# Four of twelve blocks of a gated product by Strassen's seven products on one Trainium2 core

## The chip, the core and the metric

The kernel runs on one core of a Trainium2 chip. The core has TensorE (matrix products, results in PSUM), VectorE, ScalarE and GpSimd (elementwise work), SyncE (its queue issues most DMAs), and 16 DMA engines. Each engine works through its own queue in order and waits on semaphores for the others. The metric is the device time of one execution in microseconds (us); the median of several runs counts.

## What is computed

Attention over 2 x 8 heads, then a gated feed-forward layer (this change), then a mixture of experts. The gated layer, cut from the reference:

```
rms = np.sqrt(np.mean(x * x, axis=-1, keepdims=True) + 1e-06)
xn = x / rms * rms_g                      # 1536 tokens, 512 features
g = xn @ w_gate                           # 512 x 1536
silu = g * (1.0 / (1.0 + np.exp(-g)))
val = xn @ w_val                          # 512 x 1536
return silu * val @ w_out                 # 1536 x 512
```

The weights come as 64-bit floats.

## The kernel before

**Split operands.** A float32 operand is split in two parts, hi (a rounded copy) and lo (the rest), and a product is three matmuls: hi by hi, hi by lo, lo by hi. `xh`, `xl` hold x transposed (features on partitions, four pieces k of 128) for three groups c of 512 tokens.

**The gated stage.** The 1536 gate and value features are twelve blocks i of 128. A step is a pair (i, c): `products` (L533) issues 24 matmuls of 512 columns, for z = 0 (gate) and 1 (value) twelve each (4 pieces by 3), into the PSUM tiles `ps0` and `ps1`, two buffers each. `gate1` (L556) follows one step later: VectorE multiplies `ps0` by the tokens' scale `rs` (L561), ScalarE takes SiLU (L563), VectorE multiplies by `ps1` (L565), and the result goes to `h`. So a block is 72 matmuls, and 11 blocks follow in the loop `order`.

**Unpacking.** Each weight tile of 128 x 512 comes as raw 64-bit words (`wraw`, 512 KB, `load_unit`, two buffers). `unpack` makes float32 of it in `f64t` (two buffers) and splits it: ScalarE takes the absolute value (L491); VectorE does a max (L493), an "and" with a shift (L497) and two fused operations that read the raw words and `f64t` (L499, L502); ScalarE casts to hi (L505); GpSimd subtracts for lo (L507). In a step one unit is unpacked: the gate tile of block i+1 at c = 0, the value tile at c = 1, and a tile of w_out at c = 2 (the twelve tiles of w_out, `woh` and `wol`, are done by the last block). `step1` hands the products to TensorE's queue, and then `run` interleaves the unpacking with `gate1` of the step before, one instruction group of each in turn. After it the next raw tile is loaded into the buffer just read.

**What follows.** At the last step `split_h(0)` splits 128 tokens of `h` (six casts, six subtractions). `gemm2` (L611) multiplies by w_out: per 128 tokens, twelve pieces k with three matmuls each, in order of k (L623).

**Memory.** The `big` pool holds the tiles of `woh`, `wol` (names woh0 to woh5, wol0 to wol5, two pieces each) and `h`. A later tile may take the place of an earlier one by its tag, and then waits until that one has been read.

Of the kernel before, what the change touches and what calls it, by code (L numbers as in the profile page):

```python
# [1 line left out]

# [6 lines left out]
F32 = mybir.dt.float32  # L9
# [472 lines left out]
                          s.rd[4 * k:4 * k + 4, :].rearrange("(o a) b -> o a b", o=1).to_broadcast([128, 4, 128]))  # L482


def unpack(s, raw, pool, hi, lo, eng, c=slice(0, 512)):

    nc = s.nc
    t = pool.tile([128, 512], F32, name="f64t", bufs=2)[:, c]
    raw, hi, lo = raw[:, c], hi[:, c], lo[:, c]
    b, a = raw[:, :, 0].bitcast(U32), raw[:, :, 1]  # L490
    nc.scalar.activation(t, a.bitcast(F32), AF.Abs)  # L491
    yield
    nc.vector.tensor_scalar(t, t, F64_LEAST, None, ALU.max)  # L493
# [12 lines left out]
    yield  # L506
    eng.tensor_tensor(lo, t, f(hi), ALU.subtract)  # L507


def load_unit(s, unit):  # L510

    raw = s.wpool.tile([128, 512, 2], I32, name="wraw", bufs=2)
    src = s.w_out[128 * unit[1]:128 * unit[1] + 128, :] if unit[0] == "o" else \
        s.wgv[unit[1], :, 512 * unit[2]:512 * unit[2] + 512]
    s.nc.sync.dma_start(raw.rearrange("p n t -> p (n t)"), src.bitcast(I32))
    s.wraw[unit] = raw


def split_unit(s, unit, eng, c=slice(0, 512)):
    raw = s.wraw[unit]  # L520
    if unit[0] == "o":
        hi, lo = s.woh[unit[1]], s.wol[unit[1]]
    else:
        _, i, z = unit
# [5 lines left out]
    return unpack(s, raw, s.wpool, hi, lo, eng, c)  # L530


def products(s, i, c, a, b):  # L533

    nc = s.nc
    ps = s.gp.setdefault((i, c, a, b), [])
    for z in range(2):
        if z == len(ps):
            ps.append(s.ps_g.tile([128, b - a], F32, name=f"ps{z}", bufs=2))
        p = ps[z]  # L540
        wh, wl = s.w[i, z]
# [503 lines left out]
def attn_moe_kernel(ctx, tc, qx, kx, vx, rel, ints, wgv, w_out, rms_g, w9, w9t, w1, w2, out):  # L1045
# [20 lines left out]
    s.gpool = pool(phase2, "g")  # L1066
    early = pool(phase2, "early")
    s.apool = pool(actx, "attn")
    s.xh, s.xl, s.wraw, s.w, s.rs, s.h, s.gp = {}, {}, {}, {}, {}, {}, {}

    def htiles(pool, c, qs):
        for q in qs:
# [96 lines left out]
    places = [(i, 2, 0, 512) for i in range(1, 11)] + [(11, 0, 0, 512), (11, 1, 0, 512)]  # L1169
    for n, x in enumerate(places):  # L1170
        todo.setdefault(x, []).append(("o", n))
    ahead = iter([unit for x in order for unit in todo.get(x, ())])

    mean(s, ss, 6, 12)
    some(s.first, 24)
# [11 lines left out]
        load_unit(s, next(ahead))  # L1187
    some(second, 18)
    run(products(s, 0, 2, 0, 512))
    for x in ((0, 0, 512), (1, 0, 256), (1, 256, 512)):  # L1190
        run(gate1(s, 0, *x))
    behind = [(0, 2, 0, 512)]
    rctx.close()
    actx.close()
    big = pool(phase2, "big")
    s.woh, s.wol = [], []
    for part, tiles in (("h", s.woh), ("l", s.wol)):
        for i in range(6):
            w = big.tile([128, 2, 512], F32R, name=f"wo{part}{i}", bufs=1)
            tiles += [w[:, 0, :], w[:, 1, :]]  # L1200
    htiles(big, 0, range(1, 6))
    htiles(big, 1, range(1, 6))
    htiles(big, 2, range(6))
    def step1(x, *parts):

        run(products(s, *x))
        run(*parts, *[gate1(s, *behind.pop()) for _ in behind[:1]])
        behind.append(x)

    for x in order:  # L1210
        if x == order[1]:
            octx.close()
# [12 lines left out]
    run(gate1(s, *behind.pop()))  # L1225
    phase1.close()


# [358 lines left out]
```

## Time and profile before

| | us |
|---|---|
| median of three runs | 524.77 (523.03 to 525.8) |
| the profiled execution | 523.36 |
| its span, first to last instruction | 521.4 |
| eleven blocks of the gated stage in it | 179.5 |
| granted TensorE clock, mean | 0.995 |

The span is one execution; the 2.0 us around it are not in the trace. Times in the rows below count from the span's start. A row of a timeline is start, duration, engine, line, operation, output and inputs; the bracket is how long the engine sat idle before it, and what ended that.

### The profile page before, as it was taken

What the parts mean: (1) busy time and instruction counts of PE and PEld (TensorE: products, weight loads), DVE (VectorE), ACT (ScalarE), POOL (GpSimd) and SP (SyncE); (2) the same over time, 40 slices, a digit from 0 to 9 for tenths busy, and PEclk for the clock granted to TensorE, in tenths of its full rate; (3) what the DMA queues carried; (4) which work ended last, traced back from release to release, by engine and by line L of the source; (5) the groups of instructions that cost most, each with busy time, mean ns of one, the idle gap of its engine ahead of it and who ended that gap; (6) DMA issues with size and microseconds to landing.
All of it is one profiled execution on the core that took longest, in us unless ns stands there. A gap on an engine that the chain in (4) does not pass through costs nothing.

```text
span 521.4 us, 9740 instructions
## 1 busy us (share of the span) xinstructions
PE 506.5 (97%) x3389; PEld 414.3 (79%) x3389; DVE 396.1 (76%) x989; ACT 264.9 (51%) x620; POOL 147.1 (28%) x201
## 2 busy tenths in 40 slices
PE   8999999999999999999999999999999999999993
PEld 6776878888888888888888877877898788887772
DVE  5899895688887877777764567767746899999961
ACT  3899992433333232332332525425523599888850
POOL 2577680122222122121221000000010713666001
PEclk9999999999999999999999999999999999999998
DMA  7997611323323233232227213313784699999300
GB/s 252 391 364 269 253 43 43 143 81 121 122 80 122 81 100 103 82 116 87 93 70 255 89 41 121 122 40 123 234 298 161 208 403 397 399 402 380 134 16 17
DMA packets 32417, 89.34 MB, mean 171 GB/s; under 512 B 3876, under 2 KB 4272, under 8 KB 32361
## 3 DMA queue, kind: packets, MB, share of 16 engines
q1 hardware_dynamic: 27592, 76.36, 41.1%
q0 software_dynamic: 2896, 9.14, 4.9%
q10 hardware_dynamic: 1872, 3.15, 1.7%
q8 instruction: 29, 0.48, 0.4%
q14 instruction: 28, 0.22, 0.1%
HBM read 80.93 MB, written 8.53 MB: 172 GB/s over the span
## 4 chain that ended last, share of the span: by engine, by line
PE 77%; DVE 2%; issue 1%; ACT 1%; DMA 0%; another core or an unknown queue 0%; POOLq 0%; POOL 0%; ACTq 0%
PE ps L545 34%; PE px L623 17%; PE eph L920 8%; PE epy L953 8%; PE eht L940 1%; PE lg L598 1%; PE half L545 1%; PE po L545 1%; DVE w9b L606 1%; PE pxt L589 1%; DVE hl L577 1%; PE x L1352 1%; PE eph L991 1%; PE jy L991 1%; PE ext L906 1%
## 5 line engine op out<-in xcount | busy, mean ns | idle before, releaser
L545 PE MATMUL ps<-xh,wh 128*128 128x512 f32 x272 | 106.2, 390 | 0.0
L545 PE MATMUL ps<-xl,wh 128*128 128x512 f32 x272 | 106.1, 390 | 0.0
L545 PE MATMUL ps<-xh,wl 128*128 128x512 f32 x272 | 106.0, 390 | 0.0
L880 DVE TENSOR_TENSOR ewl<-eraw,ewh 128x1024 fp32r<-128x1024 f32 x72 | 83.7, 1221 | 9.1 <-ACT ewh L871 8.9
L871 ACT CAST ewh<-eraw 128x1024 fp32r<-128x1024 f32 x72 | 71.3, 1057 | 5.1 <-DVE ewl L880 4.9
L623 PE MATMUL px<-woh,hh 128*128 128x512 f32 (+1 forms) x156 | 61.3, 393 | 0.0
L545 PEld LDWEIGHTS ps<-xh,wl 128*128 128x128 f32 x272 | 51.1, 188 | 10.5
L545 PEld LDWEIGHTS ps<-xl,wh 128*128 128x128 f32 x272 | 51.1, 188 | 10.4
L545 PEld LDWEIGHTS ps<-xh,wh 128*128 128x128 f32 x272 | 51.1, 188 | 10.3
L623 PE MATMUL px<-woh,hl 128*128 128x512 f32 (+1 forms) x156 | 58.5, 375 | 0.0
L623 PE MATMUL px<-wol,hh 128*128 128x512 f32 (+1 forms) x156 | 58.3, 373 | 0.0
L505 ACT CAST wh<-f64t 128x512 fp32r<-128x512 f32 (+1 forms) x25 | 15.1, 604 | 84.1 <-DVE f64t L502 84.1
L507 POOL TENSOR_TENSOR wl<-f64t,wh 128x512 fp32r<-128x512 f32 (+1 forms) x24 | 29.9, 1248 | 98.0 <-ACT wh L505 61.9
L493 DVE TENSOR_SCALAR f64t<-f64t 128x512 f32<-128x512 f32 (+1 forms) x37 | 36.9, 997 | 16.8 <-ACT f64t L491 16.8
L268 ACT ACTIVATE es<-es,m 128x192 f32<-128x192 f32 (+1 forms) x96 | 41.2, 434 | 4.5 <-DVE m L257 4.3
L285 POOL TENSOR_SCALAR es<-es,z 128x192 f32<-128x192 f32 (+1 forms) x94 | 36.9, 411 | 22.6 <-DVE z L277 9.4
L577 DVE TENSOR_TENSOR hl<-h,hh 128x256 fp32r<-128x256 f32 x72 | 25.4, 423 | 17.8 <-ACT hh L576 17.8
L565 DVE TENSOR_TENSOR h<-sg,ps 128x512 f32<-128x512 f32 x34 | 23.3, 684 | 19.2 <-PE ps L545 17.2
L623 PEld LDWEIGHTS px<-woh,hl 128*128 128x128 f32 x156 | 29.3, 188 | 5.6
L623 PEld LDWEIGHTS px<-woh,hh 128*128 128x128 f32 x156 | 29.4, 188 | 5.5 <-issue 0.8
L623 PEld LDWEIGHTS px<-wol,hh 128*128 128x128 f32 x156 | 29.4, 189 | 4.2
L1365 POOL DMA_INDIRECT early<-xm,si_f x1 | 1.3, 1297 | 106.8 <-DMA eraw<-in_w_dram 106.8
(234 smaller groups left out, 1004.4 us busy)
## 6 DMA issues: line engine op xcount, KB each, us to landing
eraw<-in_w_dram SPq DMA_DIRECT2D x62, 512.0 KB, 8.9
wraw<-in_wgv_dram SPq DMA_DIRECT2D x24, 512.0 KB, 3.6
vp<-in_vx_dram SPq DMA_DIRECT2D x16, 512.0 KB, 6.0
wraw<-in_w_out_dram SPq DMA_DIRECT2D x12, 512.0 KB, 3.4
eraw<-in_w_dram POOLq DMA_DIRECT2D x10, 512.0 KB, 7.0
kd<-in_kx_dram SPq DMA_DIRECT2D x7, 464.0 KB, 10.1
vp<-in_vx_dram SPq DMA_DIRECT2D x8, 384.0 KB, 4.7
xm<-x SPq DMA_DIRECT2D x12, 256.0 KB, 2.6
```

The lines of the kernel that those rows point to most:

```text
L268: nc.scalar.activation(e[:, r, e0:e0 + n], e[:, r, e0:e0 + n], AF.Exp, bias=m[:, j:j + 1], scale=-1.0, accum_out=z[:, j:j + 1])
L285: eng.tensor_scalar(e[:, r, e0:e0 + n], e[:, r, e0:e0 + n], z[:, j:j + 1], one[0], ALU.mult, *one[1:])
L493: nc.vector.tensor_scalar(t, t, F64_LEAST, None, ALU.max)
L507: eng.tensor_tensor(lo, t, f(hi), ALU.subtract)
L545: nc.tensor.matmul(p, lhsT=w[:, k, :], rhs=x[c][:, k, a:b], start=n == 0, stop=n == 11)
L565: nc.vector.tensor_tensor(u, sg, ps[1], ALU.mult)
L577: nc.vector.tensor_tensor(hl[:, i, :], src, f(hh[:, i, :]), ALU.subtract)
L623: nc.tensor.matmul(p, lhsT=h[:, k, :], rhs=w[k][:, c:c + N], start=n == 0, stop=n == 35)
L871: eng.copy(wh, raw)
L880: eng.tensor_tensor(wl, raw, f(wh), ALU.subtract)
L920: nc.tensor.matmul(self.p[half], lhsT=x[:, k, :], rhs=w[:, 512 * half:512 * half + 512], start=k == n == 0, stop=k == 3 and n == 2)
L953: nc.tensor.matmul(self.y, lhsT=h[:, k, :], rhs=w[:, c], start=n == 0, stop=n == 23)
```

## The change

In blocks 4 to 7 the groups c = 0 and c = 1 are computed together as a 2 x 2 by 2 x 2 product of blocks (gate and value by two halves of the features; two halves of the features by two token groups), in Winograd's form of Strassen's method: seven products of six matmuls instead of eight. Group c = 2 stays as it was, its 24 matmuls set between the seven.

- `Seven.blocks` builds the four sums of x's pieces, restored as hi + lo: 24 VectorE additions of 128 x 512 and 8 ScalarE casts, in 18 portions set among blocks 0 to 3.
- `Seven.sums` builds four sums of a block's weights from its two `f64t` tiles: four VectorE operations of 256 columns, a ScalarE cast and a VectorE subtraction of 1024, in the step before.
- `Seven.quad` is the block. ScalarE copies three partial sums from PSUM to PSUM (`b<-a`, `c<-a`, `d<-a`) and one to `e`, and TensorE goes on adding to the copies.
- w_out is no longer unpacked in blocks 1 to 7: two tiles in each of blocks 8, 9 and 10 and six in block 11. Its raw tiles take other tiles' places: o0 to o3 those of h05 and h15, o4, o6, o8 that of woh5, o5, o7, o9 that of wol5, o10 and o11 the ordinary buffers. A tile that takes a place in use is loaded once its forerunner has been unpacked.

The core of the diff:

```diff
-def unpack(s, raw, pool, hi, lo, eng, c=slice(0, 512)):
+def unpack(s, unit, raw, pool, hi, lo, eng, c=slice(0, 512)):
 
     nc = s.nc
-    t = pool.tile([128, 512], F32, name="f64t", bufs=2)[:, c]
+    s.full[unit] = pool.tile([128, 512], F32, name="f64t", bufs=2)
+    t = s.full[unit][:, c]
     raw, hi, lo = raw[:, c], hi[:, c], lo[:, c]
...
+SEVEN = range(4, 8)
+class Seven:
+    def __init__(self, s, big):
+        self.s, self.big, self.s7 = s, big, {}
+        self.th = [self.tile(f"th{j}", f"woh{j + 1}", F32R) for j in range(4)]
+        self.tl = [self.tile(f"tl{j}", f"wol{j + 1}", F32R) for j in range(4)]
+        self.eg = self.tile("eg", "wol5", F32)
...
+    def blocks(self):
+        s, V = self.s, self.s.nc.vector
+        m = [self.tile(f"tm{j}", tag, F32) for j, tag in enumerate(("h05", "h15", "h25", "woh5"))]
+        where = ((1, 0), (0, 0), (1, 2), (0, 2))
+        def full(j, k):
+            c, k0 = where[j]
+            V.tensor_tensor(m[j][:, k, :], f(s.xh[c][:, k0 + k, :]), f(s.xl[c][:, k0 + k, :]), ALU.add)
+        def sub(out, a, b, k):
+            V.tensor_tensor(m[out][:, k, :], m[a][:, k, :], m[b][:, k, :], ALU.subtract)
+        def high(j, out, k):
+            s.nc.scalar.copy(self.th[j][:, k, :], m[out][:, k, :])
+        def low(j, out, k):
+            V.tensor_tensor(self.tl[j][:, k, :], m[out][:, k, :], f(self.th[j][:, k, :]), ALU.subtract)
+        for j in range(4):
+            full(j, 0)
+            yield
+        for k in range(2):
+            for j in range(4 * k):
+                full(j, 1)
+                if j % 2:
+                    yield
+            sub(1, 0, 1, k)
+            yield
+            sub(0, 0, 2, k)
+            high(0, 1, k)
+            yield
+            sub(2, 2, 1, k)
+            high(2, 0, k)
+            low(0, 1, k)
+            yield
+            sub(3, 3, 2, k)
+            high(1, 2, k)
+            low(2, 0, k)
+            yield
+            high(3, 3, k)
+            low(1, 2, k)
+            yield
+            low(3, 3, k)
+            yield
+    def sums(self, i):
+        s, V = self.s, self.s.nc.vector
+        t0, t1 = (s.full["w", i, z] for z in range(2))
+        a = self.tile("s7", "woh0", F32).rearrange("p a b -> p (a b)")
+        a11, a12, a21, a22 = t0[:, 0:256], t0[:, 256:512], t1[:, 0:256], t1[:, 256:512]
+        S = [a[:, 256 * j:256 * j + 256] for j in range(4)]
+        V.tensor_tensor(S[0], a21, a22, ALU.add)
+        V.tensor_tensor(S[1], S[0], a11, ALU.subtract)
+        yield
+        V.tensor_tensor(S[2], a21, a11, ALU.subtract)
+        V.tensor_tensor(S[3], a12, S[1], ALU.subtract)
+        yield
+        tags = (("h05", "h15"), ("h25", "woh5"))[i % 2]
+        hi, lo = (self.tile(f"s7{x}", tag, F32R).rearrange("p a b -> p (a b)") for x, tag in zip("hl", tags))
+        s.nc.scalar.copy(hi, a)
+        yield
+        V.tensor_tensor(lo, a, f(hi), ALU.subtract)
+        self.s7[i] = [x.rearrange("p (j k m) -> p j k m", j=4, k=2) for x in (hi, lo)]
+        yield
+    def group(self, out, w, x, start=False):
+        n = 0
+        for k in range(2):
+            for a, b in ((w[0], x[0]), (w[0], x[1]), (w[1], x[0])):
+                self.s.nc.tensor.matmul(out, lhsT=a[:, k, :], rhs=b[:, k, :], start=start and n == 0,
+                                        stop=n == 5, skip_group_check=not start)
+                n += 1
+    def quad(self, i):
+        s, nc, V = self.s, self.s.nc, self.s.nc.vector
+        A = [[w[:, k:k + 2, :] for w in s.w[i, z]] for z in range(2) for k in (0, 2)]
+        both = self.s7.pop(i)
+        S = [[w[:, j] for w in both] for j in range(4)]
+        T = [[self.th[j], self.tl[j]] for j in range(4)]
+        X = {(c, k): [x[c][:, k:k + 2, :] for x in (s.xh, s.xl)] for c in range(2) for k in (0, 2)}
+        ua, ub = (s.h[c, i // 2][:, i % 2, :] for c in range(2))
+        e, sgb = self.eg[:, 0, :], self.eg[:, 1, :]
+        third = products(s, i, 2, 0, 512)
+        b, c, d = self.seeded
+        a = s.ps_m.tile([128, 512], F32, name="qa", tag="misc", bufs=1)
+        q = s.ps_g.tile([128, 512], F32, name="qe", tag="ps1", bufs=2)
+        self.group(a, A[0], X[0, 0], True)
+        self.group(q, S[0], T[0], True)
+        yield 0
+        nc.scalar.copy(b, a)
+        yield 1
+        nc.scalar.copy(e, q)
+        some(third, 8)
+        self.group(a, S[1], T[1])
+        yield 2
+        nc.scalar.copy(c, a)
+        self.group(b, A[1], X[0, 2])
+        yield 3
+        V.tensor_tensor(ua, b, s.rs[0], ALU.mult)
+        yield 4
+        sga = s.gpool.tile([128, 512], F32, name="sg", bufs=2)
+        nc.scalar.activation(sga, ua, AF.Silu)
+        some(third, 8)
+        self.group(a, S[2], T[2])
+        yield 5
+        nc.scalar.copy(d, a)
+        self.group(c, S[3], X[1, 2])
+        yield 6
+        V.tensor_tensor(ub, c, e, ALU.add)
+        V.tensor_tensor(e, a, e, ALU.add)
+        V.tensor_tensor(ub, ub, s.rs[1], ALU.mult)
+        yield 7
+        nc.scalar.activation(sgb, ub, AF.Silu)
+        some(third, 8)
+        self.group(d, A[3], T[3])
+        nc.gpsimd.tensor_tensor(ub, sgb, e, ALU.mult)
+        yield 8
+        V.tensor_tensor(ua, sga, d, ALU.mult)
...
+    places = [*((i, c) for i in range(8, 11) for c in (1, 2)), *((11, n // 2) for n in range(6))]
+    for n, p in enumerate(places):
+        todo.setdefault((*p, 0, 512), []).append(("o", n))
...
+    seven = Seven(s, big)
+    blocks = seven.blocks()
+    seven.seeded = [*(s.ps_n.tile([128, 512], F32, name="qb", tag="rb", bufs=2) for _ in range(2)),
+                    ps_o.tile([128, 512], F32, name="qd", tag="po", bufs=1)]
+    for x, n in (((0, 0, 512), 2), ((1, 0, 256), 1), ((1, 256, 512), 1)):
+        parts = gate1(s, 0, *x)
+        next(parts)
+        some(blocks, n)
+        next(parts, None)
+    behind = [(0, 2, 0, 512)]
+    s.gp[2, 0, 0, 512] = seven.seeded[0:2]
+    s.gp[2, 1, 0, 512] = [seven.seeded[2], s.ps_m.tile([128, 512], F32, name="qa", tag="misc", bufs=1)]
...
+    def load_o(*ns):
+        for n in ns:
+            tag = ("h05", "h15", "h05", "h15", "woh5", "wol5", "woh5", "wol5", "woh5", "wol5", None, None)[n]
+            load_unit(s, ("o", n), big if tag else None, tag)
+    after_o = {n: n + 2 for n in (0, 1, 4, 5, 6, 7)}
...
+    def step7(i):
+        q, (u0, u1) = seven.quad(i), (split(("w", i + 1, z)) for z in range(2))
+        next(q)
+        run(*[gate1(s, *behind.pop()) for _ in behind[:1]])
+        some(u0, 1)
+        some(u1, 1)
+        sums = seven.sums(i + 1) if i + 1 in SEVEN else iter(())
+        next(q)
+        some(u0, 4)
+        load_ahead()
+        next(q)
+        some(u0, 2)
+        some(u1, 4)
+        next(q)
+        load_ahead()
+        some(u1, 2)
+        some(sums, 2)
+        next(q)
+        some(sums, 1)
+        next(q)
+        third = gate1(s, i, 2, 0, 512)
+        next(third)
+        some(sums, 1)
+        next(q)
+        next(q)
+        next(q)
+        next(third, None)
+        next(q, None)
+    steps = dict(zip([(1, 0), (1, 1), (1, 2), (2, 0), (2, 1), (2, 2), (3, 0), (3, 1), (3, 2)], (1, 1, 3, 1, 1, 3, 1, 1, 9)))
...
+        i, c = x[:2]
+        if i in SEVEN:
+            if c == 0:
+                step7(i)
+                if i == 6:
+                    load_o(0, 1)
+            continue
...
-        step1(x, *[split_unit(s, unit, nc.gpsimd) for unit in todo.get(x, ())])
+        parts = [split(unit) for unit in todo.get(x, ())]
+        if (i, c) in steps:
+            parts.append(islice(blocks, steps[i, c]))
+        if (i, c) == (SEVEN[0] - 1, 2):
+            parts.append(seven.sums(SEVEN[0]))
+        step1(x, *parts)
         for unit in todo.get(x, ()):
-            unit = next(ahead, None)
-            if unit:
-                load_unit(s, unit)
+            if unit[0] == "w":
+                load_ahead()
+            elif unit[1] in after_o:
+                load_o(after_o[unit[1]])
+        if (i, c) in ((8, 2), (10, 2)):
+            load_o(*((4, 5) if i == 8 else (10, 11)))
```

## Rows read from the trace of the kernel before

**Rows 1.** The page: busy time of each engine, share of the span, instructions.
```profile
PE 506.5 (97%) x3389; PEld 414.3 (79%) x3389; DVE 396.1 (76%) x989; ACT 264.9 (51%) x620; POOL 147.1 (28%) x201
```

**Rows 2.** The chain that ended last, in order of time: start, us, what.
```profile
98.57 179.52 PE ps L545 x792
278.09 9.54 PE px L623 x42
```

**Rows 3.** Windows: us; busy (instructions) of PE, PEld, DVE, ACT, POOL; PEclk, DMA, GB/s.
```profile
163.90:180.20 16.30, 16.30 (x73) 13.51 (x72) 12.59 (x18) 5.13 (x9) 3.90 (x3) 1.00 0.30 95
261.80:278.10 16.30, 16.30 (x73) 13.50 (x72) 10.60 (x19) 6.82 (x17) 2.61 (x2) 1.00 0.22 61
```

**Rows 4.** Timeline of VectorE, one step of the stage.
```profile
174.84 0.69 DVE L565 TENSOR_TENSOR h<-sg,ps 128x512 f32<-128x512 f32 x1 [0.54 <-PE ps L545]
175.44 0.42 DVE L497 TENSOR_SCALAR f64t<-f64t 128x512 uint32<-128x512 uint32 x1
175.89 0.69 DVE L499 SCALAR_TENSOR_TENSOR f64t<-wraw,f64t 128x512 uint32<-128x512 uint32 x1
176.62 0.69 DVE L502 SCALAR_TENSOR_TENSOR f64t<-wraw,f64t 128x512 uint32<-128x512 uint32 x1
177.49 0.69 DVE L561 TENSOR_TENSOR h<-ps,rs 128x512 f32<-128x512 f32 x1 [0.17 <-PE ps L545]
178.58 1.05 DVE L493 TENSOR_SCALAR f64t<-f64t 128x512 f32<-128x512 f32 x1 [0.40 <-ACT f64t L491]
```

**Rows 5.** Timeline of ScalarE, the same step and the end of the stage.
```profile
177.34 0.62 ACT L505 CAST woh<-f64t 128x512 fp32r<-128x512 f32 x1 [3.68 <-DVE f64t L502]
177.87 0.67 ACT L491 ACTIVATE f64t<-wraw 128x512 f32<-128x512 f32 x1
178.43 0.64 ACT L563 ACTIVATE sg<-h 128x512 f32<-128x512 f32 x1
...
272.69 1.94 ACT L576 CAST hh<-h 128x256 fp32r<-128x256 f32 x6 [1.30 <-PE ps L545]
```

**Rows 6.** Timeline of GpSimd, the same step and one earlier.
```profile
178.04 1.30 POOL L507 TENSOR_TENSOR wol<-f64t,woh 128x512 fp32r<-128x512 f32 x1 [4.03 <-ACT woh L505]
...
77.68 1.01 POOL L415 TENSOR_TENSOR sq<-sq 128x256 f32<-128x256 f32 x1 [0.37 <-ACT sq L424]
```

**Rows 7.** Timeline of VectorE, earlier.
```profile
78.13 1.10 DVE L499 SCALAR_TENSOR_TENSOR f64t<-wraw,f64t 128x512 uint32<-128x512 uint32 x1
...
106.88 0.68 DVE L561 TENSOR_TENSOR h<-ps,rs 128x512 f32<-128x512 f32 x1
...
111.64 0.68 DVE L561 TENSOR_TENSOR h<-ps,rs 128x512 f32<-128x512 f32 x1
```

**Rows 8.** The tile wraw: time from DMA issue to landing.
```profile
DMA to landing us min/median/max: 3.2/3.5/3.8
```

**Rows 9.** Waits of the DMA queue of SyncE: total us, times, longest.
```profile
SPq L515 <- DVE f64t L502: 149.9, 30, 9.3
```

**Rows 10.** Timeline of VectorE, end of the stage.
```profile
273.36 2.10 DVE L577 TENSOR_TENSOR hl<-h,hh 128x256 fp32r<-128x256 f32 x6
...
278.19 0.69 DVE L565 TENSOR_TENSOR h<-sg,ps 128x512 f32<-128x512 f32 x1 [2.10 <-PE ps L545]
```

**Rows 11.** Groups by line, engine and shape: count, busy us, mean ns, idle before.
```profile
L880 DVE TENSOR_TENSOR ewl<-eraw,ewh 128x1024 fp32r<-128x1024 f32 x72 | 83.7, 1221 | 9.1 <-ACT ewh L871 8.9
L871 ACT CAST ewh<-eraw 128x1024 fp32r<-128x1024 f32 x72 | 71.3, 1057 | 5.1 <-DVE ewl L880 4.9
...
L930 ACT ACTIVATE eh<-eph 128x512 f32<-128x512 f32 x16 | 8.7, 605 | 5.5 <-issue 5.5
```

**Rows 12.** Semaphore instructions of line 565 on VectorE: ns min/median/max.
```profile
L565 DVEq EVENT_SEMAPHORE  x34: 21/21/21, 103.3 to 278.1; - x34
```

**Rows 13.** Timeline of TensorE, last product of the stage.
```profile
277.70 0.39 PE L545 MATMUL ps<-xh,wl 128*128 128x512 f32 x1
```

More of the change, by code (lines that the diff above doesn't have):

```diff
@@ L1 @@
 from contextlib import ExitStack
+from itertools import islice
 import concourse.bass as bass
@@ L507, in unpack, with load_unit @@
     eng.tensor_tensor(lo, t, f(hi), ALU.subtract)
-def load_unit(s, unit):
-    raw = s.wpool.tile([128, 512, 2], I32, name="wraw", bufs=2)
+def load_unit(s, unit, pool=None, tag=None):
+    raw = (pool or s.wpool).tile([128, 512, 2], I32, name="wraw", tag=tag or "wraw", bufs=1 if tag else 2)
     src = s.w_out[128 * unit[1]:128 * unit[1] + 128, :] if unit[0] == "o" else \
@@ L529, in split_unit @@
             s.w[i, z] = [x.rearrange("p (k m) -> p k m", k=4) for x in (hi, lo)]
-    return unpack(s, raw, s.wpool, hi, lo, eng, c)
+    return unpack(s, unit, raw, s.wpool, hi, lo, eng, c)
 def products(s, i, c, a, b):
@@ L547, in products, with tile @@
                 yield
+SEVEN = range(4, 8)
[5 more added lines that the diff above has]
+        self.eg = self.tile("eg", "wol5", F32)
+    def tile(self, name, tag, dtype):
+        return self.big.tile([128, 2, 512], dtype, name=name, tag=tag, bufs=1)
+    def blocks(self):
[108 more added lines that the diff above has]
+        V.tensor_tensor(ua, sga, d, ALU.mult)
@@ L1068, in attn_moe_kernel @@
     s.apool = pool(actx, "attn")
-    s.xh, s.xl, s.wraw, s.w, s.rs, s.h, s.gp = {}, {}, {}, {}, {}, {}, {}
+    s.xh, s.xl, s.wraw, s.full, s.w, s.rs, s.h, s.gp = {}, {}, {}, {}, {}, {}, {}, {}
     def htiles(pool, c, qs):
@@ L1168, in attn_moe_kernel @@
     todo = {(i, c, 0, 512): [("w", i + 1, c)] for i in range(1, 11) for c in range(2)}
-    places = [(i, 2, 0, 512) for i in range(1, 11)] + [(11, 0, 0, 512), (11, 1, 0, 512)]
-    for n, x in enumerate(places):
-        todo.setdefault(x, []).append(("o", n))
     ahead = iter([unit for x in order for unit in todo.get(x, ())])
+    places = [*((i, c) for i in range(8, 11) for c in (1, 2)), *((11, n // 2) for n in range(6))]
+    for n, p in enumerate(places):
+        todo.setdefault((*p, 0, 512), []).append(("o", n))
     mean(s, ss, 6, 12)
@@ L1189, in attn_moe_kernel @@
     run(products(s, 0, 2, 0, 512))
-    for x in ((0, 0, 512), (1, 0, 256), (1, 256, 512)):
-        run(gate1(s, 0, *x))
-    behind = [(0, 2, 0, 512)]
     rctx.close()
@@ L1195, in attn_moe_kernel, with split, load_ahead @@
     big = pool(phase2, "big")
[L1196 to L1203, printed above, removed]
+    s.woh, s.wol = {}, {}
+    for c in range(3):
+        htiles(big, c, range(c < 2, 5))
+    seven = Seven(s, big)
[10 more added lines that the diff above has]
+    s.gp[2, 1, 0, 512] = [seven.seeded[2], s.ps_m.tile([128, 512], F32, name="qa", tag="misc", bufs=1)]
+    def split(unit):
+        if unit[0] == "o" and unit[1] % 2 == 0:
+            for part, tiles in (("h", s.woh), ("l", s.wol)):
+                w = big.tile([128, 2, 512], F32R, name=f"wo{part}{unit[1] // 2}", bufs=1)
+                tiles[unit[1]], tiles[unit[1] + 1] = w[:, 0, :], w[:, 1, :]
+        return split_unit(s, unit, nc.gpsimd)
+    def load_ahead():
+        unit = next(ahead, None)
+        if unit:
+            load_unit(s, unit)
+    def load_o(*ns):
[3 more added lines that the diff above has]
+    after_o = {n: n + 2 for n in (0, 1, 4, 5, 6, 7)}
     def step1(x, *parts):
@@ L1208, in step1 @@
         behind.append(x)
-    for x in order:
-        if x == order[1]:
-            octx.close()
+    def step7(i):
[27 more added lines that the diff above has]
+    steps = dict(zip([(1, 0), (1, 1), (1, 2), (2, 0), (2, 1), (2, 2), (3, 0), (3, 1), (3, 2)], (1, 1, 3, 1, 1, 3, 1, 1, 9)))
+    for x in order:
+        i, c = x[:2]
[5 more added lines that the diff above has]
+            continue
+        if x == (10, 0, 0, 512):
+            for z in range(3):
+                htiles(big, z, (5,))
         if x == order[-1]:
@@ L1219, in attn_moe_kernel @@
             split_h(s, 0)
[L1220 to L1224 removed]
+        parts = [split(unit) for unit in todo.get(x, ())]
[4 more added lines that the diff above has]
+        step1(x, *parts)
+        for unit in todo.get(x, ()):
+            if unit[0] == "w":
[4 more added lines that the diff above has]
+            load_o(*((4, 5) if i == 8 else (10, 11)))
     run(gate1(s, *behind.pop()))
+    octx.close()
     phase1.close()
```

## The prediction

> **What bounds the kernel now.** I read the page first: TensorE is busy 97% of the span, every other engine well below [rows 1]. Then the chain that ended last: from 98.57 us the 792 matmuls of blocks 1 to 11 stand in it as one piece of 179.52 us, 226.7 ns each, and the w_out products follow at once, 42 in 9.54 us [rows 2]. The windows by block say the same: TensorE is full in each 16.3 us, at a granted clock of 1.00, which is the 2.4 GHz level [rows 3]. So a matmul less is worth 226.7 ns as long as nobody makes TensorE wait, and the question is who could. VectorE is next with 12.59 of 16.3 us in an ordinary block, and 10.60 in the last [rows 3].
>
> The timelines show how one step runs. VectorE does L565, L497, L499, L502, then waits 0.17 us for TensorE, does L561 and L493, and waits again [rows 4]: it keeps pace with TensorE and has about 1.2 us to spare in a step of 24 x 0.2267 = 5.44 us. Operations of 512 columns take 0.69 us and 0.42 (L497), and one may begin 0.60 us after an independent one [rows 4]. ScalarE does cast, absolute value and SiLU of 0.62 to 0.67 us, starting 0.53 to 0.56 apart [rows 5]. GpSimd's lo takes 1.30 [rows 6].
>
> Two more things are to be seen. L493 is of L497's kind and size, but took 1.05 us: it began at 178.58 while GpSimd worked from 178.04 to 179.34, and ended 0.29 after it [rows 4, 6]. L499, with two inputs in SBUF, normally 0.69, took 1.10 where GpSimd was at work until 78.69 [rows 6, 7]. So both kinds stand still until GpSimd's operation is over. Second, a raw tile lands 3.2 to 3.8 us after its issue [rows 8], and its issue waits for L502, the last reader of the buffer [rows 9]; with one unit a step and two buffers, 10.9 us apart, this is hidden before.
>
> **The change, part by part.**
>
> *Matmuls.* Seven groups of six instead of eight, in four blocks: 4 x 6 = 24 fewer, 24 x 0.2267 = -5.44 us. Operands and shapes are as before, so I keep the price.
>
> *Inside a block of seven* I lay the queues out in the order of the code, each instruction starting when its engine is free and its inputs are there (the walk). TensorE needs 66 x 0.2267 = 14.96 us. VectorE: two unpackings 2 x (0.42 + 0.42 + 0.69 + 0.69) = 4.44, seven operations of 512 columns 4.83, four of 256 at 0.42 (six, overlapping, take 2.10 [rows 10]) 1.68, one of 1024 at 1.22 [rows 11]: 12.2, and about 0.65 standing behind GpSimd: 12.9, so 2.1 us spare. ScalarE: two absolute values, two casts, three SiLUs, four copies near 0.605 and a cast of 1.06 [rows 5, 11]: 7.9 us. Each of the three copies from PSUM to PSUM ends 2.2 to 2.3 us before TensorE writes its source or adds to its copy, because eight matmuls of the third group stand between. No row has a copy that writes PSUM. The nearest are 0.605 for one reading it and, far off, 1.06 for twice the size [rows 11]; at either it is in time, so I take 0. If the cover went, TensorE would wait what the copy is late.
>
> *Preparation.* 24 additions of 0.69 (16.6 us) and 8 casts go into blocks 0 to 3; the first four fill VectorE's waits for SiLU in block 0, the rest stand where w_out's unpacking was (2.85 us a block as the rows have it [rows 4]). VectorE starts behind: its L561 at 106.88 has its twelve matmuls since 98.57 + 12 x 0.2267 = 101.3, so it is 5.6 us late, and it catches up 0.7 a step (4.76 us from L561 to L561, of 5.44) [rows 7]. With the additions it is 6.7 us behind in block 1 and 1.3 by the end of block 3. TensorE waits only when a PSUM tile of two steps ago is unread, at about 7.4 us behind: cost 0, with 0.7 to spare. The sums for block 4 are ready about 2 us before the second group of seven wants them. The loads of o0 and o1 stand in SyncE's queue until block 6 has read its sums; behind them wait only raw tiles of block 9, wanted a block later. PSUM: the banks used for the copies stood empty here.
>
> *w_out's tiles, moved.* This is where I expect the saving to go. Blocks 1 to 7 lose a unit each; blocks 8, 9, 10 have four units instead of three, and block 11 six instead of two. VectorE's work in blocks 8 to 10 is 4 x 2.22 + 6 x 0.69 = 13.0, some 1.5 standing behind GpSimd, and waits for `f64t`, which with two buffers frees only when GpSimd has made lo: about 17.1 us a block against 16.32, so it falls back 0.8 us a block. That alone is hidden.
>
> Block 11 is not. Call 0 the time at which its first matmul starts; without waits the w_out products would start at 16.32. The raw tiles of o6 to o9 pass through two places in turn. VectorE has read o5 at 0.8. Only then o7 is loaded and lands at 4.35 (3.45 after the issue). Its absolute value stands ahead of SiLU in ScalarE's queue, and SiLU ahead of L565 on VectorE: L565 of step (10, 2) ends at 6.3. Two "ands" and four fused operations follow, o7 is read at 9.35, and o9 lands at 12.9. The same again: L565 of (11, 0) ends at 14.8, o9 is read at 17.9, L561, SiLU and L565 of (11, 1) end at 19.9, while TensorE could have finished the block at 16.32. TensorE waits 1.25 us in step (11, 2), for `ps1` unread since (11, 0). The first piece of `split_h(0)`, cast at 19.45, holds the w_out products back by 1.93 more; its subtraction, behind GpSimd's lo of o9, by 0.96. The remaining pieces start 0.31 to 0.35 us apart (six in 1.94 and 2.10 [rows 5, 10]), faster than TensorE takes them. Then o10 and o11: their lo come at 27.7 and 29.0, a little after pieces 10 and 11 want them: 0.31 and 0.58. Sum 1.25 + 1.93 + 0.96 + 0.31 + 0.58 = +5.03 us. The second w_out product then finds its operands, and what is loaded after the stage waits for nothing that TensorE needs soon.
>
> What this hangs on: at a landing of 3.2 instead of 3.45 us in each turn the loss is 0.5 smaller. With GpSimd blocking nobody, 2.3 smaller. With one semaphore instruction of 21 ns [rows 12] more on each VectorE operation, 1.5 larger. L561's wait of 0.17 us after TensorE's end [rows 4], and 0.10 at the last L565 (matmul 277.70 + 0.39, start 278.19 [rows 10, 13]), are my price for a hand-over; twelve of them in the four blocks, unhidden, would be 12 x 0.17 = 2.0, and hidden 0, which I take.
>
> On the standing still, the rows give a sum of 5.03, and without it 2.7. The Trainium skill, "SBUF — State Buffer", section "Who interferes with whom", says that a VectorE operation in a two-port mode, or with two SBUF inputs against a GpSimd operation that reads SBUF, and GpSimd hold a port pair exclusively, and the second fully blocks. By that rule 5.03 holds; the rows of L493 and L499 agree with it (1.05 and 1.10 us instead of 0.42 and 0.69).
>
> **Sum.** 523.36 - 5.44 + 5.03 = 522.95 against the profiled execution. That execution lies 1.4 us under the median of the three runs, so for a median I lean a little upward: 523.5.
>
> **The rivals.**
>
> *Forecast: the saving is paid back in block 11.* 523.5, with 521 to 526 from the bounds above. For it: two places for six raw tiles, each turn some 8.5 us (from 0.8 to 9.35 to 17.9) where a step is 5.44. Against it: the chain has some 25 links, and 0.1 us on each would be 2.5 us.
>
> *VectorE keeps up, and most of the saving stays.* If the tiles of o6 to o9 were turned over a little faster and the subtractions fell between VectorE's operations, TensorE would wait 2.7 us or less; with no wait at all 523.36 - 5.44 = 517.9. So 518 to 520.7. For it: VectorE's own work in block 11 due before the w_out products is 4 x 2.22 and three `gate1` of 1.38, 13.0 us of 16.32, so the loss is order and not work. Against: the rows of L493 and L499.
>
> *VectorE becomes the bound in the four blocks of seven: slower.* Its place is the end of each block: five operations on the last groups come after the sixth group, and the next block's unpacking and sums stand behind them. It has 2.1 us to spare; from there every further microsecond costs TensorE one per block. At 3.1 (each of its 20 operations 0.155 us longer, or five more GpSimd blocks of 0.65) it costs 4 x 1.0: 527. For it: three GpSimd operations per block, one of them new, and most of VectorE's operations have two inputs in SBUF, the kind that stands still. Against: the walk shows only 0.65 of blocking.
>
> *Block 11 is worse than walked.* With the 21 ns, the 2.0 of hand-overs and the 3.8 us landing (+0.7): 522.95 + 4.2 = 527.
>
> A time outside: the removal of the 24 matmuls is a count, so 517.9 is a floor for the profile.
>
> **How the numbers follow.** I take 0.5% (2.6 us) as what a measurement of this kernel can tell from no change. Forecast 0.48, all within 0.5%. VectorE keeps up 0.27: faster. VectorE bounds the four blocks 0.13, block 11 worse than walked 0.12: slower together 0.25. Range: from 519.3, leaving out the lower half of the second case, to 527.8, a little past the 527 of the two slower ones; forecast's own 521 to 526.
>
> **What the profile after would show.** Blocks 4 to 7 of 14.96 us each, with no idle TensorE: then the first step and the hidden copies are right; longer blocks with waits on ScalarE or VectorE mean the third case. TensorE idle about 5 us in all between the last c = 2 product and the end of the first w_out product, its releasers L565, L576, L577 and L507: the forecast. VectorE's waits in block 11 should be on ScalarE's L491 and that on a DMA. Less than 3 us there would make me wrong downward, more than 8 upward. L499 and L502 with a mean above 0.69 show the blocking; if they stay at 0.69 beside GpSimd's lo, that part is wrong.

## The result, and the profile after

The changed kernel takes 526.16 us, the median of 15 runs (525.3 to 527.08), beside 523.12 for the kernel before in the same comparison (15 runs, 522.93 to 525.8). The ratio is 1.0053, 95% interval 1.0043 to 1.0063: slower by 0.5%, 3.0 us. The profiled execution has a span of 524.6 us [before 521.4] and took 526.1 us. The forecast was 523.5, no change that can be measured, and what came is a change clear of the noise. The time lies in the whole range, but just above the forecast's own 521 to 526.

The page's line of engines answers to [rows 1]:

```profile
PE 503.5 (96%) x3365; PEld 408.8 (78%) x3365; DVE 418.2 (80%) x1037; ACT 283.8 (54%) x648; POOL 153.6 (29%) x205
```

There are the 24 matmuls less, and VectorE has 22 us more to do. Where the time went is seen in the windows, one for each block, from its first matmul to the next block's first (columns as in [rows 3]). Shown are blocks 3, 5, 10 and 11:

```profile
130.81:147.13 16.32, 16.32 (x74) 13.51 (x72) 15.21 (x25) 6.30 (x10) 2.82 (x2) 1.00 0.20 64
162.31:177.51 15.20, 15.20 (x68) 12.39 (x66) 14.65 (x21) 7.74 (x14) 3.88 (x3) 1.00 0.23 71
...
240.57:256.89 16.32, 16.32 (x74) 13.51 (x72) 12.68 (x21) 6.46 (x11) 5.14 (x4) 1.00 0.10 34
256.89:278.65 21.76, 17.09 (x73) 13.17 (x71) 13.57 (x25) 7.61 (x14) 5.34 (x5) 1.00 0.35 122
```

Three things are to be seen. Blocks 1 to 3 cost what they cost before, so the preparation is hidden. The blocks of seven take 15.20 us (the first 15.18) and not 14.96, with no idle TensorE and the granted clock at 1.00: 60.78 us for the four instead of 65.28, a gain of 4.50 and not 5.44. And block 11 takes 21.76 us. TensorE's timeline shows where it stands still; the figure in brackets is its idle time (the third is that of the first matmul with w_out, the fourth that of the first one that takes `hl`):

```profile
267.54 0.39 PE L547 MATMUL ps<-xh,wl 128*128 128x512 f32 x1
268.12 0.50 PE L547 MATMUL ps<-xh,wh 128*128 128x512 f32 x1 [0.19 <-DVE h L702]
...
270.76 0.39 PE L547 MATMUL ps<-xh,wl 128*128 128x512 f32 x1
274.01 0.50 PE L547 MATMUL ps<-xh,wh 128*128 128x512 f32 x1 [2.87 <-DVE h L706]
274.35 0.39 PE L547 MATMUL ps<-xl,wh 128*128 128x512 f32 x1
...
278.65 0.50 PE L764 MATMUL px<-woh,hh 128*128 128x512 f32 x1 [1.62 <-ACT hh L717]
278.99 0.39 PE L764 MATMUL px<-wol,hh 128*128 128x512 f32 x1
280.04 0.50 PE L764 MATMUL px<-woh,hl 128*128 128x512 f32 x1 [0.66 <-DVE hl L718]
```

A wait costs a little more than its bracket, because the matmul behind it also starts late (274.01 to 274.35 instead of 0.227 later). Counted from start to start, less the 0.227 of a matmul, the places cost 0.46, 3.14, 1.90 and 0.94 us, and two more in the first w_out product (`wol` of o10 and o11) 0.25 and 0.57: 7.26 us in all. The brackets alone, with 0.29 for the last of the six, add up to 5.63.

The account, from the starts of matmuls: block 1 begins at 98.17 instead of 98.41 (-0.24), the blocks of seven -4.50, block 8 +0.02, the standing still +7.26, of which the kernel before has nothing. Sum +2.54; at the end of the w_out products the kernel is 2.64 us behind, and at the last matmul of the program 2.58. What lies behind that last matmul, 0.1 to 0.6 us, I did not follow.

The chain that ended last, in order of time, runs through block 11 like this (start, us, what):

```profile
257.84 0.70 DVE f64t L504
258.57 0.03 issue
258.60 3.80 DMA wraw<-in_w_out_dram
262.44 0.04 issue
262.48 0.66 ACT f64t L493
263.14 0.53 ACT sg L704
263.70 0.04 DVE h L706
263.74 0.56 issue
264.30 0.49 DVE f64t L499 x2
264.79 0.18 issue
264.97 1.29 DVE f64t L501 x2
266.26 0.61 DVE f64t L504
266.89 0.63 ACT woh L507
267.53 4.46 DMA wraw<-in_w_out_dram
272.02 0.04 issue
272.06 0.66 ACT f64t L493
272.72 0.53 ACT sg L704
```

That is the ring of two places as the prediction walked it: o5 read (L504), o7 landing, its absolute value (L493) ahead of SiLU (L704) and of the gate's product (L706), o7 read, o9 landing. The matmul that waited 2.87 us waits for the next L706, at 273.27. The tile `wraw` in this stretch has landings of

```profile
DMA to landing us min/median/max: 3.5/4.1/5.7
```

where [rows 8] had 3.2/3.5/3.8.

### The profile page after: what moved, and what is told of

Read it like the earlier page. It is cut to its first block, busy times and chain, and to the rows that moved or that the text cites. A ratio compares the mean times of both kernels' runs of the same rounds, so it can differ in the third digit from the quotient of the medians.

```text
span 524.6 us, 9769 instructions
## 1 busy us (share of the span) xinstructions
PE 503.5 (96%) x3365; PEld 408.8 (78%) x3365; DVE 418.2 (80%) x1037; ACT 283.8 (54%) x648; POOL 153.6 (29%) x205
## 4 chain that ended last, share of the span: by engine, by line
PE 39%; DVE 5%; issue 2%; DMA 2%; ACT 2%; POOL 1%; another core or an unknown queue 0%; POOLq 0%; ACTq 0%; SPq 0%
PE px L764 16%; PE eph L1061 9%; PE epy L1094 8%; DMA wraw<-in_w_out_dram 2%; DVE hl L718 1%; PE lg L739 1%; PE eht L1081 1%; DVE w9b L747 1%; DVE f64t L501 1%; PE pxt L730 1%; PE x L1565 1%; PE eph L1132 1%; PE jy L1132 1%; PE ext L1047 0%; POOL wol L509 0%
## 5 line engine op out<-in xcount | busy, mean ns | idle before, releaser
L547 PE MATMUL ps<-xh,wh 128*128 128x512 f32 x192 | 75.4, 393 | 3.1 <-DVE h L706 2.9
L547 PE MATMUL ps<-xh,wl 128*128 128x512 f32 x192 | 75.0, 391 | 0.0
L547 PE MATMUL ps<-xl,wh 128*128 128x512 f32 x192 | 75.0, 391 | 0.0
L509 POOL TENSOR_TENSOR wl<-f64t,wh 128x512 fp32r<-128x512 f32 (+1 forms) x24 | 31.7, 1319 | 100.6 <-ACT wh L507 70.2
L547 PEld LDWEIGHTS ps<-xh,wh 128*128 128x128 f32 x192 | 36.0, 188 | 11.1 <-DVE h L706 3.3
L547 PEld LDWEIGHTS ps<-xh,wl 128*128 128x128 f32 x192 | 36.1, 188 | 7.5
L547 PEld LDWEIGHTS ps<-xl,wh 128*128 128x128 f32 x192 | 36.1, 188 | 7.3
L495 DVE TENSOR_SCALAR f64t<-f64t 128x512 f32<-128x512 f32 (+1 forms) x37 | 24.4, 662 | 18.4 <-ACT f64t L493 18.2
L718 DVE TENSOR_TENSOR hl<-h,hh 128x256 fp32r<-128x256 f32 x72 | 26.7, 440 | 11.3 <-ACT hh L717 11.3
L493 ACT ACTIVATE f64t<-wraw 128x512 f32<-128x512 f32 (+1 forms) x37 | 23.6, 651 | 11.4 <-DMA wraw<-in_w_out_dram 6.0
```

What stands on the lines that cost most here:

```text
L718: nc.vector.tensor_tensor(hl[:, i, :], src, f(hh[:, i, :]), ALU.subtract)
```

## Experiments

**e1: half of w_out.** The second half of w_out's tiles isn't loaded or taken apart, and pieces 6 to 11 of the w_out products use the tiles of 0 to 5; everything else is the changed kernel. The values after the stage, and with them the routing, are others, so only the stage is read.

```
-    for n, p in enumerate(places):
+    for n, p in enumerate(places[:6]):
...
+            for n in range(6):
+                s.woh[n + 6], s.wol[n + 6] = s.woh[n], s.wol[n]
```

> The six units of w_out in block 11 are left out: pieces 6 to 11 of the w_out products read the tiles of pieces 0 to 5, so the values behind the stage differ, the routing sees other data, and only the gated stage and the first w_out product are to be read. Theory A (the loss is the late unpacking in block 11): TensorE has no gap over 0.3 us from the first product of block 1 to the end of the first w_out product; the stage and that product together take 4.5 us less than before, instead of 2.8 us more. Theory B (the loss is made before block 11, in the blocks of seven or by VectorE's lag): gaps of 3 us or more stay.

Its block 11, 256.95 to 273.27, takes 16.32 us with TensorE busy throughout, and no matmul of the stage or of the w_out products waits. The last of the w_out products starts at 390.99 us instead of 398.32: 7.3 us earlier than in the changed kernel. So what the change loses there comes with the six units of w_out in block 11, all of it. The six units in blocks 8 to 10 are still taken apart here, and by themselves they cost nothing.

**e2: without the copies in PSUM.** The three copies b, c, d are left out and each group starts its PSUM tile afresh, so the sums are not handed over and the values are others; only the blocks of seven are read.

```
-        nc.scalar.copy(b, a)
...
-        self.group(b, A[1], X[0, 2])
+        self.group(b, A[1], X[0, 2], True)
...
```

> In the blocks of seven the three copies from PSUM to PSUM are left out, and the groups that would add to a copy start afresh, so the values are others and only blocks 4 to 7 are read. They took 15.2 us each after the change, 14.96 at 226.7 ns a matmul. Theory C (the hand-overs from ScalarE cost this, with every wait met in time): they fall to 14.96 to 15.0. Theory D (it comes from something else, such as the other operands or the change of group): they stay at 15.2, to 0.05.

The blocks take 15.20 us as with the copies, and each matmul has the same distance to the next as in the changed kernel, to 2 ns. So the 0.24 us a block is no hand-over of the copies and no wait for ScalarE's copies. (This run's block 1 begins 2.7 us late, before anything that the edit touches; its 528.58 us says nothing of the copies.) The copies themselves take 0.57 to 0.58 us, just under the nearer of my two bounds, and are hidden.

**e3: the move alone.** Blocks 4 to 7 with eight products as before, but w_out's tiles late and in two places, as in the changed kernel; the preparation runs and is not used.

```
-        if i in SEVEN:
-            if c == 0:
-                step7(i)
...
-            continue
...
```

> Blocks 4 to 7 are ordinary again (72 matmuls, no sums of weights); x's four sums are still built and w_out is unpacked as late as in the change. Theory A: the move alone costs its 7.2 us: 523.1 + 7 = 530, 528 to 531, with TensorE idle about 7 us in block 11 and the first w_out product. Theory B: within 1.5 us of before, 523 to 524.5.

529.91 us (529.14 to 530.56), ratio 1.0124 (1.0105 to 1.0143), before 523.06: the move costs 6.9 us by itself. It has TensorE's clock to show as well. Windows from block 11's start to the end of its long wait, and from there to the first w_out product:

```profile
261.54:277.89 16.35, 13.76 (x62) 11.07 (x60) 9.09 (x17) 5.44 (x9) 3.89 (x3) 1.00 0.47 161
277.89:282.53 4.64, 4.61 (x13) 3.32 (x13) 3.94 (x8) 2.19 (x5) 1.49 (x2) 0.63 0.00 2
```

After a wait of 2.59 us the granted clock is 0.63, so the 1.2 GHz level in part of the stretch, and seven matmuls in a row come 0.43 us apart. In the changed kernel's profile it stayed at 1.00 after 2.87 us. It did not make the first w_out product late: that took 20.99 us from block 11's start here and 21.76 there, and here too TensorE waited for the first cast piece of `h` (idle for 0.04 us in front of it). That this is one kernel's single profile against another's leaves open what decides the clock.

**e4: four places.** o6 and o7 get places of their own and are loaded in block 8, so only o8 and o9 wait for a place.

```
-            tag = (... "woh5", "wol5", "woh5", "wol5", "woh5", "wol5", None, None)[n]
+            tag = (... "woh5", "wol5", "woh4", "wol4", "woh5", "wol5", None, None)[n]
...
-    after_o = {n: n + 2 for n in (0, 1, 4, 5, 6, 7)}
+    after_o = {0: 2, 1: 3, 4: 8, 5: 9}
...
-            load_o(*((4, 5) if i == 8 else (10, 11)))
+            load_o(*((4, 5, 6, 7) if i == 8 else (10, 11)))
```

> o6 and o7 get places of their own (those of woh4 and wol4, free after block 7), so that o6 to o9 are loaded a block or a step earlier; order and work of all engines stay. Theory A, ring part (most of the loss is the wait for o7 and o9 to land): gaps in block 11 and the first w_out product fall from 7.25 to about 3.5 us, 526.2 - 3.7 = 522.5, 521.5 to 523.5. If the loss is VectorE's work in block 11 and not the landing: within 1 us of 526.2.

522.77 us (522.26 to 523.32), ratio 0.9991 (0.9981 to 1.0001): 3.4 us under the changed kernel's 526.16, which is what the ring of two places was worth. Both waits for PSUM tiles are gone. What is left, TensorE's groups by line from 256 to 300 us (busy, mean ns | idle before, releaser):

```profile
L764 PE MATMUL px<-woh,hh 128*128 128x512 f32 x32 | 12.9, 403 | 1.5 <-ACT hh L717 1.5
L764 PE MATMUL px<-wol,hh 128*128 128x512 f32 x32 | 12.7, 397 | 0.3 <-POOL wol L509 0.3
L764 PE MATMUL px<-woh,hl 128*128 128x512 f32 x31 | 12.2, 394 | 0.7 <-DVE hl L718 0.7
```

are the waits for the first pieces of h.

**e5: the gate first.** Two places as in the change, but in blocks 8 to 11 the queues get the gate operations ahead of the unit of w_out.

```
-        run(*parts, *[gate1(s, *behind.pop()) for _ in behind[:1]])
+        gate = [gate1(s, *behind.pop()) for _ in behind[:1]]
+        run(*(gate + list(parts) if x[0] >= 8 else list(parts) + gate))
```

> The changed kernel with one order turned round: in blocks 8 to 11 VectorE and ScalarE get the gate operations of the step before first and the unit of w_out behind them. The two places of o4 to o9 stay. Theory A (in block 11 the loss is order: SiLU and the product with it stand behind an absolute value that waits for a late raw tile, so a late load also holds TensorE's PSUM tiles): TensorE no longer waits in block 11, about 3.7 us of the 7.25 go, 526.2 - 3.7 = 522.5, range 521.5 to 523.5. Rival B (the ring itself is the limit, whoever stands first: a raw tile is then read later, o7 and o9 land later, and what block 11 gains the first w_out products lose): 525 to 527, with the waits moved from ps1 to the pieces of w_out.

521.26 us (521.11 to 522.39), ratio 0.9962 (0.9949 to 0.9975), a little below the range expected. The tiles are late as before, but nothing that TensorE needs stands behind them: the waits for `ps1` are gone, and 3.1 us are left in front of the pieces of h and of `wol`.

**e6: both.**

> Both at once: four places for o4 to o9 and the gate ahead of the unit in blocks 8 to 11. Theory A (the two causes are the whole of the loss in block 11): with four places alone 3.5 us of TensorE's gaps are left between the last product and the first w_out products, of which the walk leaves 0 to 0.5 with both; 522.8 - 3.0 to 3.5 = 519.3 to 519.8, range 518.8 to 520.5, faster than the kernel before by about 3.5 us. It doesn't reach 518.0, because the blocks of seven stay at 15.2 us. Rival B (VectorE's work in block 11 is the limit, and order only moves the wait): 522 to 523, with the same 3.5 us of gaps, now in front of the pieces of w_out's last tiles.

519.0 us (518.58 to 519.87), ratio 0.9924 (0.9911 to 0.9938). Block 11 is full again:

```profile
256.97:273.29 16.32, 16.32 (x73) 13.52 (x72) 13.72 (x27) 9.29 (x19) 5.99 (x5) 1.00 0.28 96
```

VectorE has 13.72 us of work there, as much as with the waits (13.57): it was never too much work. The order and the places were the whole of the 7.26 us.

**e7 to e10: what makes the blocks of seven 15.20.** e7 gives every group of six the first group's operands; e8 is the kernel before with the two PSUM tiles of a product taking turns every 6 matmuls. In e7, e9 and e10 the values of these blocks are others, so only the length of the blocks is read and not the time.

```
+        A = [[w[:, 0:2, :] for w in s.w[i, 0]] for _ in range(4)]
+        S = A
+        T = [[x[0][:, 0:2, :] for x in (s.xh, s.xl)] for _ in range(4)]
+        X = {(c, k): T[0] for c in range(2) for k in (0, 2)}
...
```

> Only the stage of blocks 4 to 7 is to be read: every group of six there takes the same weights and the same piece of x (those of the first group), so the sums and x's restored pieces are made and not used and the values of these blocks are others. Order, PSUM tiles, copies and waits of the groups stay. Theory A (the 0.24 us that each block of seven takes beyond 66 x 226.7 ns comes from its operands, where they lie in SBUF): the blocks fall to 14.96. Rival B (it comes from how short the runs of matmuls into one PSUM tile are, six and eight instead of twelve): they stay at 15.20.

```
+    runs = (range(2), range(2, 4)) if i else (range(4),)
+    order = [(z, k) for ks in runs for z in range(2) for k in ks]
+    for z, k in order:
...
```

> The kernel before with one edit, which leaves the result as it is: in blocks 1 to 11 the two PSUM tiles of a product take turns every 6 matmuls instead of every 12. Theory B (short runs into one PSUM tile cost TensorE time): a block takes more than 16.32 us, at the cadence of the blocks of seven 72 x 230.3 ns = 16.58, so 11 x 0.26 = +2.9 us, 526 (525 to 527). Rival A (the operands, not the runs): 16.32 us a block and 523.1 (522.5 to 523.8).

e7's blocks of seven take 14.96 us:

```profile
192.20:207.16 14.96, 14.96 (x67) 12.39 (x66) 10.82 (x16) 6.89 (x13) 3.90 (x4) 1.00 0.21 71
```

In e8 blocks 2 to 11 stay at 16.32. Its time, 524.13 us (524.02 to 527.39), is 0.9 above the kernel before, not the expected 2.9: block 1 alone takes 17.33, with a wait of 0.7 for a PSUM tile that is now wanted six matmuls earlier. Short runs cost nothing; the operands do. Which of them, with e6 as the base:

```
-        T = [[self.th[j], self.tl[j]] for j in range(4)]
+        T = [[x[c][:, k:k + 2, :] for x in (s.xh, s.xl)] for c in range(2) for k in (0, 2)]
```

> Only the stage of blocks 4 to 7 is to be read (the values there are others). The kernel with four places and the gate first; its groups take pieces of x itself where they took x's restored pieces, and keep the weights' sums. Theory A1 (the restored pieces as moving operand cost the 0.24 us a block): 14.96 to 15.0 us a block. Rival A2 (the sums of weights as stationary operand cost it): still 15.15 to 15.20. If both carry a part, in between.

```
-        S = [[w[:, j] for w in both] for j in range(4)]
+        S = A
```

> Only the stage of blocks 4 to 7 is to be read (the values there are others). The same kernel; its groups take pieces of w itself where they took sums of pieces, and keep x's restored pieces. Theory A1 (the restored pieces cost it): still 15.15 to 15.20 us a block. Rival A2 (the sums of weights cost it): 14.96 to 15.0.

With x in place of the restored pieces 15.01 us, with w in place of the sums still 15.20. So x's restored pieces, `th` and `tl`, carry 0.19 of the 0.24 as the moving operand, and the sums of weights at most the other 0.05; in e10 the matmuls of all four groups with the restored pieces come 233 ns apart.

**e11 and e12: the same tiles 64 and 32 bytes further.** One line on top of e6; e12 has 8 instead of 16 columns.

```
     big = pool(phase2, "big")
+    big.tile([128, 16], F32, name="pad", bufs=1)
```

> The kernel with four places and the gate first, and one unused tile of 64 bytes per partition between the first two tiles of the pool big and the rest. By the program's memory layout x's restored pieces and the sums of weights begin 32 bytes into a block of 128 bytes, x's own pieces and w's 96 bytes in; the 64 bytes bring all of them to 96. Theory A (what costs the 0.24 us a block is that the two operands of a matmul, or of one and the next, begin at different places of such a block): the blocks of seven fall to 14.96, and 519.0 falls by 4 x 0.24 to 518.0, range 517.5 to 518.6. Rival B (it is that the restored pieces lie in another region of SBUF than x, or what they hold): 15.20 us a block and 519.0.

> The same with 32 bytes instead of 64: the restored pieces and the sums of weights begin 64 bytes into a block of 128, x's and w's own pieces 96 bytes in. Theory A: still more than 15.0 us a block of seven, since the operands still begin at different places. Rival B: 15.20 too. If it falls to 14.96 here as well, the difference of place is not what counts.

e11 takes 517.62 us (517.39 to 520.02), ratio 0.989 (0.9871 to 0.9909), before 523.64 there. TensorE's timeline on the same group, first of the changed kernel, then of e11:

```profile
176.11 0.39 PE L639 MATMUL qd<-th,wh 128*128 128x512 f32 x1
176.34 0.39 PE L639 MATMUL qd<-tl,wh 128*128 128x512 f32 x1
176.57 0.39 PE L639 MATMUL qd<-th,wl 128*128 128x512 f32 x1
176.81 0.39 PE L639 MATMUL qd<-th,wh 128*128 128x512 f32 x1
...
177.51 0.39 PE L639 MATMUL qa<-xh,wh 128*128 128x512 f32 x1
```

```profile
175.86 0.39 PE L639 MATMUL qd<-th,wh 128*128 128x512 f32 x1
176.09 0.39 PE L639 MATMUL qd<-tl,wh 128*128 128x512 f32 x1
176.32 0.39 PE L639 MATMUL qd<-th,wl 128*128 128x512 f32 x1
176.54 0.39 PE L639 MATMUL qd<-th,wh 128*128 128x512 f32 x1
...
177.22 0.39 PE L639 MATMUL qa<-xh,wh 128*128 128x512 f32 x1
```

Six matmuls take 177.51 - 176.11 = 1.40 us, 233 ns each, in the one, and 177.22 - 175.86 = 1.36, 227 ns, in the other. The whole block is at 14.96:

```profile
177.22:192.18 14.96, 14.96 (x67) 12.39 (x66) 14.45 (x21) 7.55 (x13) 3.87 (x3) 1.00 0.35 111
```

With 32 bytes it isn't (the same block of e12, a single execution of 521.09 us; its block 1 began 2.3 us later than e11's, before anything that the edit touches, so that time is not compared):

```profile
179.98:195.21 15.23, 15.23 (x68) 12.39 (x66) 14.08 (x20) 7.52 (x14) 4.01 (x4) 1.00 0.34 113
```

So it is where the operands begin, not the region that they lie in and not what they hold: with x, w, the restored pieces and the sums all 96 bytes into a block of 128 the cadence (start to start) is 227 ns; with 32 or 64 for some and 96 for the others it is not. The places are read from the program's memory layout, not from a trace, and only these shifts were tried. By the same layout `woh` and `hh` both begin 32 bytes in, and the w_out products of the changed kernel come 227 ns apart (284.50, 284.73, 284.95): 32 by itself is not slow. Why TensorE minds is open.

## Why the prediction failed

The mechanism was the one forecast, the saving paid back in block 11, but it paid back more than the saving. Two terms of the sum were wrong: the saving was put 0.94 us too large, and the cost of block 11 was put 2.23 us too small. With both as measured the sum is 523.36 - 4.50 + 7.26 = 526.12, the time of the profiled execution; the small entries of the account above cancel.

*Matmuls, -5.44.* The step "operands and shapes are as before, so I keep the price" failed: it measured -4.50. Shapes were as before, but the moving operand of four groups in seven is a new tile in a new place, and in the last group, with w itself against it, the matmuls come 233 ns apart (at a place 64 bytes on, 227). I had looked for the risk here in hand-overs and VectorE's pace; e2 shows that the hand-overs of the copies cost nothing. My sign for this step knew only blocks of 14.96 us, or longer ones with waits; longer ones without a wait were not foreseen.

*Block 11, +5.03.* It measured 7.26. Place by place: the wait for `ps1` in step (11, 2) was put at 1.25 and cost 3.14; a wait of 0.46 one step earlier was not foreseen; the first cast 1.93 and 1.90; the subtraction behind GpSimd 0.96 and 0.94; o10 and o11 0.89 and 0.82. So all but the ring are right to 0.1 us, and the ring was 2.35 short. Its parts: VectorE has read o5 at 258.53, 1.64 us after block 11's start, where I had 0.8. The landing of o7 took 3.80 and that of o9 4.46, where I took 3.45 for each. Together 2.2. So the step that failed is the turn of the ring: the landing above all, 1.36 of the 2.2, and the place at which it begins. [rows 8] are of tiles loaded one at a time, one a step of 5.44 us, and here they go in company. Behind o7's load (258.60) those of o10 and o11 are issued (259.02, 259.49), and o9's (267.53) follows o8's (266.92), since VectorE reads o6 and o7 in one go. The 4.46 lies outside the 3.2 to 3.8 of [rows 8]; the 3.80 is their top, so that o7's load was slowed by the two behind it is not shown. That the company is the cause is read from rows and not from an experiment: in the same profile a load issued 0.42 us behind another (at 224.38) landed after 4.55, and one issued 0.48 behind two (at 259.49) after 5.74. That the walk has the right structure, e4 and e5 show: 3.7 us was expected of either remedy, and in the profiles 3.7 and 4.2 of the 7.26 us went (3.4 and 4.9 of the medians). My sign for the forecast, about 5 us of idle TensorE with four named releasers, was met too, by brackets of 5.63 us on the same four lines and L702 (0.19); it was too coarse to tell 5.03 from 7.26.

*VectorE falls back 0.8 us a block in 8 to 10.* The first gate operation of each block starts at 211.25, 228.51 and 245.83, 17.26 and 17.32 apart, in blocks of 16.32 to 16.34: 0.9 to 1.0 a block. That is a little more than the 0.8 forecast, and part of why o5 was read late.

*Preparation 0, copies 0, loads of o0 and o1 hidden.* Right: blocks 1 to 3 at 16.32, no wait in blocks 4 to 7.

*Standing still beside GpSimd.* Rows of VectorE in the changed kernel, the first two from a block of seven:

```profile
167.26 1.79 DVE L501 SCALAR_TENSOR_TENSOR f64t<-wraw,f64t 128x512 uint32<-128x512 uint32 x1
...
170.62 1.52 DVE L623 TENSOR_TENSOR s<-f64t 128x256 f32<-128x256 f32 x1
...
259.79 1.06 DVE L495 TENSOR_SCALAR f64t<-f64t 128x512 f32<-128x512 f32 x1 [0.66 <-ACT f64t L493]
263.17 0.43 DVE L495 TENSOR_SCALAR f64t<-f64t 128x512 f32<-128x512 f32 x1 [2.32 <-ACT f64t L493]
...
278.94 2.72 DVE L718 TENSOR_TENSOR hl<-h,hh 128x256 fp32r<-128x256 f32 x6
```

GpSimd works on lo from 167.22 to 168.51, from 170.57 to 171.86, from 259.27 to 260.57 and from 277.17 to 279.70. L501 takes 1.79 beside it instead of 0.69, L623 1.52 instead of 0.42, L495 1.06 and alone 0.43, and six subtractions 2.72 instead of the 2.10 of [rows 10]. The Trainium skill, "SBUF — State Buffer", section "Who interferes with whom", by which one of the two fully blocks the other, agrees with these rows. Of the 0.94 us that TensorE lost at the first subtraction about 0.6 is this standing still. The sign that I had named for the blocking (L499 and L502 before, L501 and L504 now, longer than 0.69) is met in all four blocks of seven: L501 took 1.8 us beside GpSimd in blocks 4 to 6 and L504 1.67 in block 7. In block 11 neither meets GpSimd, and they keep their 0.69.

*The rivals.* VectorE was nearer to being the bound in the blocks of seven than I had it: 14.0 to 14.7 us busy of 15.20 in blocks 4 to 6, not 12.9. The cause is the standing still: 2.2 to 2.8 us in each of these blocks (in block 5, 1.10 at L501, 1.10 at L623 and 0.64 at L495), where the walk showed 0.65. It cost nothing, and even at 14.96 in e11 the 14.45 fit; but of the 2.1 us that I held to be spare 0.6 to 1.1 were left, so that this rival stayed away is in part luck. VectorE keeping up, the faster case, is what e6 makes of it by order and places. Block 11 worse than walked, to which I gave 0.12, is what came. Its +0.7 for slower landings was about half of the 1.36 that they cost; its 2.0 for hand-overs did not come, as no matmul waits in the blocks of seven; and no rival had the price of the matmuls.

*The lean.* The 0.55 us that I added for a median rested on three executions with a median of 524.77. That of 15 is 523.12, below the profiled execution, so the lean had no ground, and only by luck does it make the miss smaller.

## What to carry to other kernels

Work that is moved later is priced by the landing that it will see then: tiles whose places come free in pairs load in pairs, and in this ring each of the two late landings was paid. In a queue in order, put what the bound engine waits for ahead of what waits for a transfer; the same 13.6 to 13.7 us of VectorE's work cost 7.26 us or nothing. And a new operand in a new place is not "as before" until the cadence of its matmuls has been read. The version with four places, the gate first and the shift of 64 bytes, 517.62 us, beats both kernels: 1.1% below the one before.

## What the runs showed that I had not expected

- Matmuls of 512 columns come 227 ns apart or 233 with nothing waiting and the granted clock at 1.00, by where their operands begin: a shift of 64 bytes took 0.24 us off a block of 66 (0.19 off the first) and 0.9 us off the stage.
- A load of 512 KB alone in its queue (issued at 253.13) lands after 3.5 us; with two others issued within 0.9 us behind it, after 3.80, the top of [rows 8]; 0.6 us behind another, after 4.46; as the third of three, after 5.74.
- An operation of VectorE with two inputs in SBUF, begun 0.04 us after one of GpSimd, took 1.79 us instead of 0.69, and ended 0.5 us after GpSimd had.
- After a wait of 2.6 us TensorE's granted clock was 0.63 over the next 4.6 us in e3, after one of 2.9 us it was 1.00 in the changed kernel.
- ScalarE copies a tile of 128 x 512 from PSUM to PSUM in 0.57 us, less than the 0.605 of reading one [rows 11].
